# Attention scores of six half sequences: two heads at once in TensorE's row halves

## The chip, the cores and the metric

The kernel runs on one core of a Trainium2 chip. The metric is the time of one execution on the device in microseconds (us), lower is better. Before the change it is 242.82 us, the median of three runs (242.07 to 243.31); the profiled execution has a span of 239.8 us.

A core has five engines that run beside each other: TensorE (PE) multiplies matrices, VectorE (DVE), ScalarE (ACT) and GpSimd (POOL) work on elements, and SyncE (SP) mostly starts transfers. Each takes its instructions in program order, and waits on semaphores where it needs another engine's result. TensorE writes into PSUM, which here is cut into eight banks of 128 x 512 fp32; ScalarE and VectorE read them.

## What is computed

Attention with a local window and a few global keys, and then a feed-forward layer with two gates on its result:

```python
def _attn_ref(q, k, v, n_global, n_local):          # q, k, v: 4 x 8 heads x 768 x 64
    scores = scale * np.matmul(q, k.transpose(0, 1, 3, 2))
    ...
    keep = is_global | is_local                     # 8 global keys, the last 96 keys
    bias = -slopes[:, None, None] * dist[None, :, :]
    scores = np.where(keep, scores + bias[None, :, :, :], -1000000000.0)
    a = softmax(scores)
    return np.matmul(a, v)

def _moe_ref(x, w_gate, w_val, w_out):              # x: 3072 x 512, inner width 1536
    gate = np.maximum(x @ w_gate, 0.0)
    return gate * (x @ w_val) @ w_out
```

## The kernel before, in words

**Halves.** Each of the four sequences of 768 positions is cut into two halves of 384 queries; the kernel numbers them s = 0 to 7, and this text says half one to half eight. Half one is s = 0. The feed-forward layer of a half c has 24 products of its first stage (a gate and a value product for each of 12 blocks, L700: four matmuls of 384 columns each), then the second stage (L733 in full, or L590, which forms the product of two row blocks from seven smaller products, with sums of h and of weights that VectorE makes, L556 and L583 to L586). ScalarE applies the relu to a gate product (L709), VectorE multiplies the value product by it (L716, `ht`).

**The weave.** There is no scheduler: engines run in the order in which the code records instructions. `weave` goes through the feed-forward products of half c and records, at set fractions of their number, the pieces of attention of half c+1 (`attention_pieces`) and of the preparation of half c+2 (`early_pieces`). So a TensorE instruction of an attention piece that waits holds up all feed-forward products behind it. Halves one and two are done by other functions in a start-up section. Half three's pieces lie in the products of halves one and two, half four's to seven's in 0.88 of the products of the half before, half eight's in 0.8 of them.

**Attention of a half.** Heads come in pairs p = 0 to 3, with e = 0, 1 for the head in the pair. Keys lie in tiles j of 128 rows, the 8 global keys first. A half touches four or five tiles, each with w of 128 query columns in three groups; they are sorted into three groups g of a PSUM bank each (`banks_of_half`).
- *Scores* (`piece_qk`, L410): both heads of a pair in one matmul. The 128 rows of the stationary operand are the keys of both heads, 64 dimensions each. The queries `qTb` are padded: for e = 0 rows 64 to 127 are zero, for e = 1 rows 0 to 63. The result has 2·3·w columns. One bank of the pool `qk_psum` (three banks) per group.
- *Exp* (L413) reads the bank and writes `es` as bf16; *masks* (`piece_mask`, L428) multiply it on VectorE with the bias factors. The masks of one piece are recorded behind the exp of the next.
- *Values* (`piece_av`, L444): four or five matmuls per head into a bank of `av_psum` (two banks, in turn). 64 of their rows are the values, 64 the sums of weights. ScalarE takes the logarithm of the sums (L453), and after the second head of a pair the inverse by an exp (L458, `rcp`).
- *Normalization* (`piece_norm`, L464): VectorE multiplies each head's values by `rcp` into `xT`. This frees the head's `av_psum` bank.

The feed-forward products take the other three banks (`ff_psum`).

**Order of pieces.** For a half, `attention_pieces` gives 26 pieces: scores of pairs 0 and 1 (three pieces each), values of pair 0 (two), its second normalization, scores of pair 2, values of pair 1, and so on. Each scores piece records one group's matmuls and its exp.

**Preparation** (`early_pieces`): GpSimd casts keys and queries to bf16 (L366, L374; the query casts go into the padded `qz`), transposing transfers bring them to `kNb` and `qTb` (L377, L381), and GpSimd puts keys in their order (`piece_order`). For half three, TensorE transposes (`T2_piece`), and ScalarE copies the queries into the padded layout (L312).

Of the kernel before, what the change touches and what calls it, by code (L numbers as in the profile page):

```python
# [8 lines left out]
FP32 = mybir.dt.float32  # L9
BF16 = mybir.dt.bfloat16  # L10
FP16 = mybir.dt.float16
AF = mybir.ActivationFunctionType
# [4 lines left out]
def kernel(  # L17
# [12 lines left out]
    nc = tc.nc  # L30

    B, H, S, D = q.shape
    NG = int(n_global)
    NL = int(n_local)
    DM = H * D
# [3 lines left out]
    HP = H // 2  # L39
    QH = S // 2  # L40
    NN = 3
    KT = 128 - NG
    PK = KT // NN
    WQ = 72
    NHALF = 2 * B
    NT = -(-S // KT)
    scale = 1.0 / math.sqrt(D)
# [5 lines left out]
    banks_of_half = [[], []]  # L53
    spans = []
    for half in range(2):
        for j in range(NT):
            w0 = PK * j - 128 * half
            a, b_ = max(0, w0), min(128, w0 + WQ)
# [7 lines left out]
    const = ctx.enter_context(tc.tile_pool(name="const", bufs=1))  # L66
    setupp = ctx.enter_context(tc.tile_pool(name="setupp", bufs=1))
    stage = ctx.enter_context(tc.tile_pool(name="stage", bufs=1))
    es_pool = ctx.enter_context(tc.tile_pool(name="es", bufs=3))
    rc_pool = ctx.enter_context(tc.tile_pool(name="rc", bufs=2))  # L70
    xt_pool = ctx.enter_context(tc.tile_pool(name="xt", bufs=3))
    ht_pool = ctx.enter_context(tc.tile_pool(name="ht", bufs=2))
# [14 lines left out]
    kT = [[const.tile([128, NT, 128], BF16, name=f"kT{i}_{p}") for p in range(HP)] for i in range(2)]  # L87
    qTb = [const.tile([128, HP, 2, QH], BF16, name=f"qT{i}") for i in range(2)]
    kNb = [const.tile([128, HP, QH], BF16, name=f"kN{i}") for i in range(2)]
    qz = [const.tile([128, NN, HP, 2, 128], BF16, name=f"qz{i}") for i in range(2)]  # L90
    kc = [const.tile([128, NN, DM], BF16, name=f"kc{i}") for i in range(2)]

    obuf = const.tile([128, 2, 5, DM // 2], FP32)
# [7 lines left out]
    m_all = const.tile([128, H, 2, NN, WQ], BF16)  # L101
# [141 lines left out]
    def warm_up(n):  # L243
        wps = ff_psum.tile([128, 512], FP32, name="ff_ps")
        for _ in range(n):
            nc.tensor.matmul(wps, lhsT=warm, rhs=warm.unsqueeze(1).to_broadcast([128, 4, 128]), start=True, stop=True)

    xT_of = {}
    es_of = {}
    es01_of = {}  # L250
    av_of = {}

    cast_of = {}
# [55 lines left out]
    def piece_copy_q(s, p, copy=nc.vector.tensor_copy):  # L309
        for e in range(2):  # L310
            r = slice(64 * e, 64 * e + 64)
            copy(qTb[s % 2][r, p, e, :], tp_of[s, p, 0][r, :])  # L312
# [32 lines left out]
    def piece_exp(s, p, g):  # L345
        if p == HP - 1:

            es = kNb[s].rearrange("d p t -> d (p t)")[:, 480 * g : 480 * (g + 1)]
        else:
            if g == 0:  # L350
                es01_of[s, p] = es_pool.tile([128, 2, 480], BF16, name="es01")
            es = es01_of[s, p][:, g] if g < 2 else es_pool.tile([128, 480], BF16, name="es2")
        c = 0
        for j, a, w, m in banks_of_half[s % 2][g]:
            for e in range(2):
                es_of[s, p, j, e] = (es, c)
                c += NN * w
        nc.scalar.activation(es[:, 0:c], qk_of[s, p][g][:, 0:c], AF.Exp, bias=0.0, scale=scale)  # L358
# [3 lines left out]
        for g in range(3):  # L362
            piece_exp(s, p, g)

    def piece_cast_k(s, p):
        nc.gpsimd.tensor_copy(  # L366
            kc[s % 2].rearrange("t n (h d) -> t h n d", d=D)[:, 2 * p : 2 * p + 2],
            ks_of[s][:, 2 * p : 2 * p + 2, :].rearrange("t e (n d) -> t e n d", n=NN))

    def piece_cast_q(s, p):  # L370

        qsrc = qs_of[s][:, 2 * p : 2 * p + 2, :].rearrange("t e (n d) -> t e n d", n=NN)
        for e in range(2):
            nc.gpsimd.tensor_copy(qz[s % 2][:, :, p, e, 64 * e : 64 * e + 64], qsrc[:, e])  # L374

    def piece_xk(s, n):
        nc.sync.dma_start_transpose(  # L377
            out=kNb[s % 2][:, :, n * 128 : (n + 1) * 128], in_=kc[s % 2][:, n])

    def piece_xq(s, n):  # L380
        nc.sync.dma_start_transpose(  # L381
            out=qTb[s % 2].rearrange("d p e t -> d (p e) t")[:, :, n * 128 : (n + 1) * 128],
            in_=qz[s % 2][:, n].rearrange("t p e z -> t (p e z)"))

    def piece_order(s, p):
        b, half = divmod(s, 2)
        put_keys(nc.gpsimd.tensor_copy, nc.gpsimd.tensor_copy, kT[b % 2][p], kNb[s % 2][:, p], half)

    def early_pieces(s):
        out = [(0.0, lambda p=p: piece_cast_k(s, p)) for p in range(HP)]  # L390
        out += [(0.0, lambda n=n: piece_xk(s, n)) for n in range(NN)]
        out += [(0.0, lambda p=p: piece_cast_q(s, p)) for p in range(HP)]
        out += [(0.0, lambda n=n: piece_xq(s, n)) for n in range(NN)]
        out += [(0.0, lambda p=p: piece_order(s, p)) for p in range(HP)]
        return out

    def piece_qk(s, p, g, later=None):
        b, half = divmod(s, 2)
        kt = kT[b % 2][p]
        qd = qTb[s % 2][:, p].rearrange("d e (n p) -> d e n p", n=NN)  # L400
        bank = banks_of_half[half][g]
        cols = sum(2 * NN * w for _, _, w, _ in bank)
        ps = qk_psum.tile([128, 512], FP32, name="qk_ps")
        if g == 0:
            es01_of[s, p] = es_pool.tile([128, 2, 480], BF16, name="es01")
        es = es01_of[s, p][:, g] if g < 2 else es_pool.tile([128, 480], BF16, name="es2")
        c = 0
        for j, a, w, m in bank:
            n_ = 2 * NN * w
            nc.tensor.matmul(ps[:, c : c + n_], lhsT=kt[:, j, :],  # L410
                             rhs=qd[:, :, :, a : a + w], start=True, stop=True)
            c += n_
        nc.scalar.activation(es[:, 0:cols], ps[:, 0:cols], AF.Exp, bias=0.0, scale=scale)  # L413
        if later is None:
            piece_mask(s, p, bank, es)
        else:
            later.append(lambda: piece_mask(s, p, bank, es))
# [15 lines left out]
    def piece_av(s, p, e):  # L433
        b, half = divmod(s, 2)
        h = 2 * p + e
        vb = vbuf[b % 2]
        av = av_psum.tile([128, 512], FP32, name="av_ps")
        av_of[s, p, e] = av
        av3 = av[:, 0:QH].rearrange("d (n p) -> d n p", n=NN)
        todo = [t for bank in banks_of_half[half] for t in bank]  # L440
        for i, (j, a, w, m) in enumerate(todo):
            es, c = es_of[s, p, j, e]
            z0 = 2 * D * h + (D if e == 0 else 0)
            nc.tensor.matmul(av3[:, :, a : a + w],  # L444
                             lhsT=vb[:, j, z0 : z0 + 128],
                             rhs=es[:, c : c + NN * w].rearrange("k (n p) -> k n p", n=NN),
                             start=(i == 0), stop=(i == len(todo) - 1),
                             skip_group_check=True)
        o0, d0 = (0, 64) if e == 0 else (64, 0)
        if e == 0:  # L450
            av_of[s, p, "l"] = rc_pool.tile([128, QH], FP32, name="lnd")
        ln = av_of[s, p, "l"]
        nc.scalar.activation(ln[o0 : o0 + 64], av[d0 : d0 + 64, 0:QH], AF.Ln, bias=0.0, scale=1.0)  # L453
        if e == 1:
            if s not in xT_of:
                xT_of[s] = xt_pool.tile([128, N_DC, QH], BF16, name="xT")
            rc = rc_pool.tile([128, QH], FP32, name="rcp")
            nc.scalar.activation(rc, ln, AF.Exp, bias=0.0, scale=-1.0)  # L458
            av_of[s, p, "r"] = rc
            piece_norm(s, p, 0)  # L460
# [43 lines left out]
    def piece_mul_wide(s, p):  # L504
        if s not in xT_of:
            xT_of[s] = xt_pool.tile([128, N_DC, QH], BF16, name="xT")
        nc.vector.tensor_tensor(xT_of[s][:, p, :], av_of[s, p][1][:, 0:QH], av_of[s, p, "r"], op=ALU.mult)  # L507

    def attention_pieces(s):
        masks = []  # L510

        def qk(p, g):
            ready = masks[:]
            masks.clear()
            piece_qk(s, p, g, masks)
            for f in ready:
                f()

        def flush():
            for f in masks:  # L520
                f()
            masks.clear()

        QK = lambda p: [(0.18, lambda g=g: qk(p, g)) for g in range(3)]
        AV = lambda p: [(0.29, lambda e=e: (flush(), piece_av(s, p, e))) for e in range(2)]
        N = lambda p: [(0.0, lambda: piece_norm(s, p, 1))]
        g = QK(3)
        a = AV(2)
        return (QK(0) + QK(1) + AV(0) + N(0) + QK(2) + AV(1) + N(1) + g[0:1] + a[0:1] + g[1:3] + a[1:2]
                + N(2) + [(0.0, lambda: None)] * 2 + AV(3) + N(3))  # L530


    out_v = out.rearrange("(s p n) d -> s n p d", p=128, n=NN)
# [156 lines left out]
    def ffn_pieces(c):  # L690
# [63 lines left out]
        if c == NHALF - 2:  # L754
            return f1, pair.items({"1": late[0:2], "2": late[2:4]})

        space = qz[0].rearrange("t n p e z -> t (n p e z)").bitcast(FP16)
        across = Pair((c - 1, 2), (c, 2), space.rearrange("t (s c z) -> t s c z", s=4, c=NP))
        sums = across.sums(0, NP)
        return f1, (pair.items({"1": late[0:2], "2": late[2:4], "4": sums[0:1], "6": sums[1:2], "5": sums[2:4]})  # L760
# [32 lines left out]

    for h in range(H):
        setup_sid(h)
    QKB, FFB, AVB = (qk_psum, "qk_ps"), (ff_psum, "ff_ps"), (av_psum, "av_ps")

    def AV(s, p, *pools):
        piece_av_wide(s, p, *pools)
        piece_norm_wide(s, p)  # L800
# [130 lines left out]
        nc.gpsimd.memset(kT[1][p][:, 3, 32:128].bitcast(mybir.dt.uint32), 0)  # L931
        nc.gpsimd.memset(kT[1][p][:, 6, NG + 48 : 128].bitcast(mybir.dt.uint32), 0)
    nc.gpsimd.memset(vbuf[1][:, NT - 1, :].bitcast(mybir.dt.uint32), 0)
    for i in range(2):
        nc.gpsimd.memset(qz[i].rearrange("t n p e z -> t (n p e z)").bitcast(mybir.dt.uint32), 0)
    for j in range(NT):
        fill_ones(nc.gpsimd, 1, j)
    for p in range(HP):
# [3 lines left out]
    def T2_piece(p):  # L942
        piece_t(2, p, *QKB, apart=True)
        piece_copy_k(2, p)
        piece_copy_q(2, p, nc.scalar.copy)

    T2 = [(0.0, lambda p=p: T2_piece(p)) for p in range(HP)]
    weave(f1_1[G[0]] + f1_0[G[1]][4:] + f1_1[G[1]],
# [54 lines left out]
```

The softmax here doesn't subtract the row's maximum and nothing guards it: scores larger than these inputs give would overflow.

## Time and profile before

| engine | busy, us | share of the span |
|---|---|---|
| TensorE matmuls | 232.1 | 97% |
| VectorE | 174.8 | 73% |
| ScalarE | 154.3 | 64% |
| GpSimd | 95.6 | 40% |

| group | count | mean of one, ns |
|---|---|---|
| gate and value products, 128 x 384 (L700) | 768 | 326 |
| scores (L410) | 118 | 286 |
| values (L444) | 216 | 226 |
| exp of scores, 128 x 432 (L413) | 38 | 531 |
| logarithm (L453) | 48 | 485 |
| inverse (L458) | 24 | 523 |
| normalization (L464) | 48 | 555 |
| h product (L716) | 96 | 554 |

The mean of a matmul is its time from start to end; the next one starts before it ends, so counts times means is more than TensorE's busy time. Busy time alone doesn't say what bounds: for that the chain of waits is read, which goes back from the last instruction to what released each one. TensorE's granted clock is 1.00 over the whole span. In the timeline a row is a start, a duration, the engine, the line and the tiles, and in brackets the idle time ahead of it and what ended it.

### The profile page before, as it was taken

The numbers are of one execution on the slowest core, as the hardware profiler recorded it, in microseconds if no ns is written. First come the engines' busy times: TensorE is split into PE (matmuls) and PEld (weight loads), VectorE is DVE, ScalarE is ACT, GpSimd is POOL, SyncE is SP. The second block draws the span as 40 slices with busy tenths as digits, with TensorE's granted clock in tenths as the row PEclk, the third lists the DMA queues.
The fourth block names the chain that finished last, engine by engine and source line by source line (L and its number), as shares of the span: only waits on it lengthen the run. The fifth ranks groups of instructions, "written<-read, shape, count | busy, mean of one in ns | idle before, by whom it ended". The sixth has DMA issues, their size and how long they took to land.

```text
span 239.8 us, 5192 instructions
## 1 busy us (share of the span) xinstructions
PE 232.1 (97%) x1859; PEld 155.9 (65%) x1859; DVE 174.8 (73%) x443; ACT 154.3 (64%) x328; POOL 95.6 (40%) x213
## 2 busy tenths in 40 slices
PE   7889999999999999999999999999999999999992
PEld 3676756666558666766658666676658666866682
DVE  6878676767877778585985778675985867964783
ACT  7899856878662787548754787547764888433300
POOL 8998935915590068103484066502460000000000
PEclk9999999999999999999999999999999999999999
DMA  6999999997989946938569756929451200020004
GB/s 171 197 173 185 205 282 261 171 103 253 129 178 148 305 122 133 93 94 258 92 112 128 224 159 154 110 68 290 69 131 45 90 0 3 0 87 3 0 26 151
DMA packets 78329, 32.37 MB, mean 135 GB/s; under 512 B 55424, under 2 KB 76928, under 8 KB 78304
## 3 DMA queue, kind: packets, MB, share of 16 engines
q0 software_dynamic: 34896, 10.27, 38.1%
q1 hardware_dynamic: 43408, 21.78, 34.3%
q8 instruction: 14, 0.23, 0.4%
q14 instruction: 11, 0.09, 0.1%
HBM read 28.38 MB, written 6.29 MB: 145 GB/s over the span
## 4 chain that ended last, share of the span: by engine, by line
PE 89%; ACT 4%; DMA 2%; DVE 1%; SPq 1%; issue 0%; DVEq 0%; ACTq 0%
PE ff_ps L700 51%; PE ff_ps L590 15%; PE ff_ps L733 9%; PE qk_ps L410 6%; PE av_ps L444 6%; DMA qs<-in_q_dram 2%; ACT es L358 2%; SPq L116 1%; PE av_ps L479 1%; PE qk_ps L296 1%; ACT es L413 1%; PE qk_ps L479 1%; DVE obuf L601 0%; ACT kN L358 0%; ACT grelu L709 0%; DVE xT L507 0%
## 5 line engine op out<-in xcount | busy, mean ns | idle before, releaser
L700 PE MATMUL ff_ps<-xT,wv 128*128 128x384 bf16 x384 | 77.7, 326 | 0.1
L700 PE MATMUL ff_ps<-xT,wg 128*128 128x384 bf16 x384 | 77.7, 325 | 0.0
L709 ACT ACTIVATE grelu<-ff_ps 128x384 bf16<-128x384 f32 x96 | 46.9, 491 | 45.3 <-PE ff_ps L700 32.6
L716 DVE TENSOR_TENSOR ht<-ff_ps,grelu 128x384 f16<-128x384 f32 x96 | 53.1, 554 | 24.4 <-PE ff_ps L700 12.8
L700 PEld LDWEIGHTS <-wv 128*128 128x128 bf16 x384 | 36.2, 97 | 22.3 <-DMA wv<-in_moe_w_val_dram 0.4
L700 PEld LDWEIGHTS <-wg 128*128 128x128 bf16 x384 | 36.0, 97 | 20.9 <-issue 0.5
L464 DVE TENSOR_TENSOR xT<-av_ps,rcp 64x384 bf16<-64x384 f32 x48 | 26.7, 555 | 24.9 <-ACT rcp L458 24.0
L413 ACT ACTIVATE es<-qk_ps 128x432 bf16<-128x432 f32 (+2 forms) x78 | 40.9, 534 | 5.5 <-PE qk_ps L410 3.5
L428 DVE TENSOR_TENSOR es<-es,m_all 128x432 bf16<-128x432 bf16 (+5 forms) x118 | 32.9, 322 | 0.2
L366 POOL CAST kc<-ks 128x384 bf16<-128x384 f32 x20 | 9.4, 517 | 57.9 <-DMA ks<-in_k_dram 57.9
L453 ACT ACTIVATE lnd<-av_ps 64x384 f32<-64x384 f32 x48 | 23.3, 485 | 8.9 <-PE av_ps L444 8.5
L410 PE MATMUL qk_ps<-qT,kT 128*128 128x432 bf16 (+5 forms) x118 | 26.6, 286 | 0.1
L151 POOL DMA_DIRECT2D vbuf<-in_v_dram x29 | 24.8, 863 | 0.1
L601 DVE TENSOR_TENSOR obuf<-ff_ps,obuf 128x512 f32<-128x512 f32 (+1 forms) x35 | 20.5, 592 | 4.3 <-PE ff_ps L590 2.0
L733 PE MATMUL ff_ps<-wo_sb,ht 128*128 128x512 f16 x96 | 22.8, 378 | 0.0
L444 PEld LDWEIGHTS <-vbuf 128*128 128x128 bf16 x216 | 18.3, 98 | 6.8
L444 PE MATMUL av_ps<-es,vbuf 128*128 128x216 bf16 (+4 forms) x216 | 21.4, 226 | 0.0
L590 PEld LDWEIGHTS <-hsum 128*128 128x128 f16 x168 | 16.4, 98 | 2.0
L410 PEld LDWEIGHTS <-kT 128*128 128x128 bf16 x118 | 11.4, 98 | 7.7
L590 PE MATMUL ff_ps<-wo_sum,hsum 128*128 128x256 f16 x126 | 14.9, 273 | 0.0
L590 PEld LDWEIGHTS <-ht 128*128 128x128 f16 x144 | 13.7, 97 | 1.8
L733 PEld LDWEIGHTS <-ht 128*128 128x128 f16 x96 | 8.7, 97 | 8.7
(125 smaller groups left out, 245.7 us busy)
## 6 DMA issues: line engine op xcount, KB each, us to landing
out_dram<-obuf SPq DMA_DIRECT2D x22, 256.0 KB
ks<-in_k_dram SPq DMA_DIRECT2D x5, 768.0 KB
qs<-in_q_dram SPq DMA_DIRECT2D x5, 768.0 KB
vbuf<-in_v_dram POOLq DMA_DIRECT2D x23, 120.0 KB, 4.8
wv<-in_moe_w_val_dram POOLq DMA_DIRECT2D x3, 512.0 KB, 9.8
wo_sb<-in_moe_w_out_dram POOLq DMA_DIRECT2D x1, 1536.0 KB, 21.1
wg<-in_moe_w_gate_dram POOLq DMA_DIRECT2D x2, 512.0 KB, 9.7
ks<-in_k_dram SPq DMA_DIRECT2D x4, 192.0 KB
```

The lines of the kernel that those rows point to most:

```text
L151: nc.gpsimd.dma_start(out=v_dst(b, NG + r0, NG + r0 + n, j), in_=v[b, :, KT * j + r0 : KT * j + r0 + n, :].rearrange("h p d -> p h d"))
L410: nc.tensor.matmul(ps[:, c : c + n_], lhsT=kt[:, j, :], rhs=qd[:, :, :, a : a + w], start=True, stop=True)
L413: nc.scalar.activation(es[:, 0:cols], ps[:, 0:cols], AF.Exp, bias=0.0, scale=scale)
L428: nc.vector.tensor_mul(e4, e4, mk)
L444: nc.tensor.matmul(av3[:, :, a : a + w], lhsT=vb[:, j, z0 : z0 + 128], rhs=es[:, c : c + NN * w].rearrange("k (n p) -> k n p", n=NN), star ...
L453: nc.scalar.activation(ln[o0 : o0 + 64], av[d0 : d0 + 64, 0:QH], AF.Ln, bias=0.0, scale=1.0)
L464: nc.vector.tensor_tensor(xT_of[s][r, p, :], av_of[s, p, e][r, 0:QH], av_of[s, p, "r"][r], op=ALU.mult)
L590: nc.tensor.matmul(ps[:, c0 : c0 + DH], lhsT=lhs(i), rhs=rhs(i), start=(i == 0), stop=(i == NP - 1), skip_group_check=True)
L700: nc.tensor.matmul(st[key][:, 0:QH], lhsT=w_of(w, dc, fc), rhs=xT_of[c][:, dc, :], start=(dc == 0), stop=(dc == N_DC - 1))
L709: nc.scalar.activation(gr, psg[:, 0:QH], AF.Relu, bias=0.0, scale=1.0)
L716: nc.vector.tensor_tensor(ht[:, fc, :], psv[:, 0:QH], st["r", fc], op=ALU.mult)
L733: nc.tensor.matmul(ps2, lhsT=ht[:, fc, n * 128 : (n + 1) * 128], rhs=wo_sb[:, fc, :], start=(fc == 0), stop=(fc == N_FC - 1))
```

## The change

For halves three to eight the scores are no longer formed from a pair's 128 rows with padded queries. Each head's 64 rows are a matmul of their own, on rows 0 to 63 for e = 0 and 64 to 127 for e = 1, with the queries of that head alone (3·w columns instead of 2·3·w). The two matmuls of a pair use different row halves of TensorE and write different banks, so they can run at the same time. That is what it is for: to spare TensorE the zero half of the padded products.

A unit of scores (`score_unit`) now covers two groups for two banks each, four PSUM banks: one of `av_psum` and the three of `qk_psum`. There are three units per half, each recorded in one piece, and 12 exps, one per bank, in pieces of their own (`unit_exp`). A bank holds the same head e of two pairs (heads 4pp + e and 4pp + e + 2) instead of both heads of one pair; the masks take the two heads with a step of two. The order of a half's pieces becomes 27:

```
X(U0) X X X wait X(U1) X X a0 X a0 N0 X(U2) X a1 X X a1 N1 AV2 N2 wait wait AV3 N3
```

where X(Uk) records unit k and the first of its exps, X another exp, a0 and a1 the values of one head of pairs 0 and 1, AV both heads, N the second normalization. The queries lose their padding: one cast per pair instead of two on GpSimd, half the bytes in the query transposes, one copy instead of two in `T2_piece`, no zeroing of `qz`. The exp tiles become a pool of 12 buffers of 128 x 480.

```diff
-    es_pool = ctx.enter_context(tc.tile_pool(name="es", bufs=3))
+    es_pool = ctx.enter_context(tc.tile_pool(name="es", bufs=12))
...
-    qz = [const.tile([128, NN, HP, 2, 128], BF16, name=f"qz{i}") for i in range(2)]
+    qT2 = [qTb[1].rearrange("d p e t -> d (p e t)")[:, i * HP * QH : (i + 1) * HP * QH].rearrange(
+        "d (p t) -> d p t", p=HP) for i in range(2)]
+    qc = [const.tile([128, NN, DM], BF16, name=f"qc{i}") for i in range(2)]
...
+    def score_unit(s, groups, pools):
+        b, half = divmod(s, 2)
+        out = []
+        for pp, g in groups:
+            banks = []
+            for e in range(2):
+                pool, name = pools.pop(0)
+                banks.append(pool.tile([128, 512], FP32, name=name))
+                out.append((pp, g, e, banks[e]))
+            c = 0
+            for j, a, w, m in banks_of_half[half][g]:
+                for p in (2 * pp, 2 * pp + 1):
+                    for e in range(2):
+                        r = slice(64 * e, 64 * e + 64)
+                        q3 = qT2[s % 2][r, p].rearrange("d (n p) -> d n p", n=NN)
+                        nc.tensor.matmul(banks[e][:, c : c + NN * w], lhsT=kT[b % 2][p][r, j, :],
+                                         rhs=q3[:, :, a : a + w], start=True, stop=True)
+                    c += NN * w
+        return out
...
-        QK = lambda p: [(0.18, lambda g=g: qk(p, g)) for g in range(3)]
...
-        return (QK(0) + QK(1) + AV(0) + N(0) + QK(2) + AV(1) + N(1) + g[0:1] + a[0:1] + g[1:3] + a[1:2]
-                + N(2) + [(0.0, lambda: None)] * 2 + AV(3) + N(3))
+        U = [([(0, 0), (0, 1)], (AVB, QKB, QKB, QKB)),
+             ([(0, 2), (1, 0)], (AVB, QKB, QKB, QKB)),
+             ([(1, 1), (1, 2)], (AVB, QKB, QKB, QKB))]
+        X = lambda u=None: [(0.0, lambda: x(u))]
...
+        return (X(U[0]) + X() + X() + X() + wait + X(U[1]) + X() + X() + a0[0:1] + X() + a0[1:2] + N(0)
+                + X(U[2]) + X() + a1[0:1] + X() + X() + a1[1:2] + N(1) + AV(2) + N(2) + wait * 2 + AV(3) + N(3))
...
-    for i in range(2):
-        nc.gpsimd.memset(qz[i].rearrange("t n p e z -> t (n p e z)").bitcast(mybir.dt.uint32), 0)
...
-        piece_copy_q(2, p, nc.scalar.copy)
+        nc.scalar.copy(qT2[0][:, p], tp_of[2, p, 0])
```

More of the change, by code (lines that the diff above doesn't have):

```diff
@@ L246, in warm_up @@
             nc.tensor.matmul(wps, lhsT=warm, rhs=warm.unsqueeze(1).to_broadcast([128, 4, 128]), start=True, stop=True)
+    QKB, FFB, AVB = (qk_psum, "qk_ps"), (ff_psum, "ff_ps"), (av_psum, "av_ps")
     xT_of = {}
     es_of = {}
-    es01_of = {}
     av_of = {}
@@ L349, in piece_exp @@
         else:
-            if g == 0:
-                es01_of[s, p] = es_pool.tile([128, 2, 480], BF16, name="es01")
-            es = es01_of[s, p][:, g] if g < 2 else es_pool.tile([128, 480], BF16, name="es2")
+            es = es_pool.tile([128, 480], BF16, name="es")
         c = 0
@@ L363, in piece_biased, with piece_cast2, piece_x @@
             piece_exp(s, p, g)
-    def piece_cast_k(s, p):
+    def piece_cast2(s, p, dst, src):
         nc.gpsimd.tensor_copy(
[L367 to L383, printed above, removed]
+            dst[s % 2].rearrange("t n (h d) -> t h n d", d=D)[:, 2 * p : 2 * p + 2],
+            src[s][:, 2 * p : 2 * p + 2, :].rearrange("t e (n d) -> t e n d", n=NN))
+    def piece_x(dst, src, n):
+        nc.sync.dma_start_transpose(out=dst[:, :, n * 128 : (n + 1) * 128], in_=src[:, n])
     def piece_order(s, p):
@@ L389, in early_pieces @@
     def early_pieces(s):
[L390 to L393, printed above, removed]
+        out = [(0.0, lambda p=p: piece_cast2(s, p, kc, ks_of)) for p in range(HP)]
+        out += [(0.0, lambda n=n: piece_x(kNb[s % 2], kc[s % 2], n)) for n in range(NN)]
+        out += [(0.0, lambda p=p: piece_cast2(s, p, qc, qs_of)) for p in range(HP)]
+        out += [(0.0, lambda n=n: piece_x(qT2[s % 2], qc[s % 2], n)) for n in range(NN)]
         out += [(0.0, lambda p=p: piece_order(s, p)) for p in range(HP)]
@@ L403, in piece_qk @@
         ps = qk_psum.tile([128, 512], FP32, name="qk_ps")
-        if g == 0:
-            es01_of[s, p] = es_pool.tile([128, 2, 480], BF16, name="es01")
-        es = es01_of[s, p][:, g] if g < 2 else es_pool.tile([128, 480], BF16, name="es2")
+        es = es_pool.tile([128, 480], BF16, name="es")
         c = 0
@@ L507, in piece_mul_wide, with unit_exp, mask @@
         nc.vector.tensor_tensor(xT_of[s][:, p, :], av_of[s, p][1][:, 0:QH], av_of[s, p, "r"], op=ALU.mult)
-    def attention_pieces(s):
[L510 to L517, printed above, removed]
+    def score_unit(s, groups, pools):
[17 more added lines that the diff above has]
+        return out
+    def unit_exp(s, pp, g, e, ps):
+        bank = banks_of_half[s % 2][g]
+        cols = sum(2 * NN * w for _, _, w, _ in bank)
+        es = es_pool.tile([128, 480], BF16, name="es")
+        nc.scalar.activation(es[:, 0:cols], ps[:, 0:cols], AF.Exp, bias=0.0, scale=scale)
+        def mask():
+            c = 0
+            for j, a, w, m in bank:
+                n_ = 2 * NN * w
+                e4 = es[:, c : c + n_].rearrange("k (i n p) -> k i n p", i=2, n=NN)
+                h0 = 4 * pp + e
+                mk = m_all[:, h0 : h0 + 3 : 2, 0 if j == 0 else 1, :, m : m + w]
+                if w == WQ:
+                    e4 = e4.rearrange("k i n p -> k i (n p)")
+                    mk = mk.rearrange("k i n p -> k i (n p)")
+                nc.vector.tensor_mul(e4, e4, mk)
+                for i in range(2):
+                    es_of[s, 2 * pp + i, j, e] = (es, c + i * NN * w)
+                c += n_
+        return mask
+    def attention_pieces(s):
+        masks, units = [], []
         def flush():
@@ L522, in flush, with scores, x @@
             masks.clear()
-        QK = lambda p: [(0.18, lambda g=g: qk(p, g)) for g in range(3)]
-        AV = lambda p: [(0.29, lambda e=e: (flush(), piece_av(s, p, e))) for e in range(2)]
+        def scores(groups, pools):
+            units.extend(score_unit(s, groups, list(pools)))
+        def x(scored=None):
+            ready = masks[:]
+            masks.clear()
+            if scored:
+                scores(*scored)
+            masks.append(unit_exp(s, *units.pop(0)))
+            for f in ready:
+                f()
+        U = [([(0, 0), (0, 1)], (AVB, QKB, QKB, QKB)),
+             ([(0, 2), (1, 0)], (AVB, QKB, QKB, QKB)),
+             ([(1, 1), (1, 2)], (AVB, QKB, QKB, QKB))]
+        X = lambda u=None: [(0.0, lambda: x(u))]
+        AV = lambda p: [(0.0, lambda e=e: (flush(), piece_av(s, p, e))) for e in range(2)]
         N = lambda p: [(0.0, lambda: piece_norm(s, p, 1))]
-        g = QK(3)
-        a = AV(2)
-        return (QK(0) + QK(1) + AV(0) + N(0) + QK(2) + AV(1) + N(1) + g[0:1] + a[0:1] + g[1:3] + a[1:2]
-                + N(2) + [(0.0, lambda: None)] * 2 + AV(3) + N(3))
+        wait = [(0.0, lambda: None)]
+        a0, a1 = AV(0), AV(1)
+        return (X(U[0]) + X() + X() + X() + wait + X(U[1]) + X() + X() + a0[0:1] + X() + a0[1:2] + N(0)
+                + X(U[2]) + X() + a1[0:1] + X() + X() + a1[1:2] + N(1) + AV(2) + N(2) + wait * 2 + AV(3) + N(3))
     out_v = out.rearrange("(s p n) d -> s n p d", p=128, n=NN)
@@ L755, in ffn_pieces @@
             return f1, pair.items({"1": late[0:2], "2": late[2:4]})
-        space = qz[0].rearrange("t n p e z -> t (n p e z)").bitcast(FP16)
+        space = qTb[0].rearrange("d p e t -> d (p e t)").bitcast(FP16)
         across = Pair((c - 1, 2), (c, 2), space.rearrange("t (s c z) -> t s c z", s=4, c=NP))
@@ L795 @@
         setup_sid(h)
-    QKB, FFB, AVB = (qk_psum, "qk_ps"), (ff_psum, "ff_ps"), (av_psum, "av_ps")
     def AV(s, p, *pools):
```

## The prediction

> **What bounds the kernel now.** I read the busy table first, then the chain that ended last, then the costliest groups, and last the timeline around the places that the change touches.
>
> ```profile
> PE 232.1 (97%) x1859; PEld 155.9 (65%) x1859; DVE 174.8 (73%) x443; ACT 154.3 (64%) x328; POOL 95.6 (40%) x213
> ...
> PE 89%; ACT 4%; DMA 2%; DVE 1%; SPq 1%; issue 0%; DVEq 0%; ACTq 0%
> ...
> L410 PE MATMUL qk_ps<-qT,kT 128*128 128x432 bf16 (+5 forms) x118 | 26.6, 286 | 0.1
> ```
>
> TensorE is the bound: 89% of the chain, and from 22 us to 235 us the chain is nothing but its matmuls. The 286 ns of a score matmul (L410) is latency and overlaps the next one; its cost is the spacing of starts. Four 384-column matmuls of a gate or value product take 0.65 us (the rows at 144.29 and 144.93 below), 2.36 columns per ns, issue included. From 45 to 236 us I compared all starts with that rate: 189.4 us of matmul and 0.85 us of anything else. So TensorE has no slack: work taken off it shortens the kernel, and every wait put in front of it lengthens it.
>
> The change gives TensorE new waits on the accumulator banks of the values product (AVB, two banks), so the chain that frees such a bank matters. In half six (timeline, 144 us; start, duration):
>
> ```profile
> 143.98 0.47 PE L444 MATMUL av_ps<-es,vbuf 128*128 128x72 bf16 x5
> 144.29 0.81 PE L700 MATMUL ff_ps<-xT,wg 128*128 128x384 bf16 x4
> 144.48 0.48 ACT L453 ACTIVATE lnd<-av_ps 64x384 f32<-64x384 f32 x1 [0.26 <-PE av_ps L444]
> 144.93 0.81 PE L700 MATMUL ff_ps<-xT,wv 128*128 128x384 bf16 x4
> 145.00 0.52 ACT L458 ACTIVATE rcp<-lnd 128x384 f32<-128x384 f32 x1
> 145.55 0.55 DVE L464 TENSOR_TENSOR xT<-av_ps,rcp 64x384 bf16<-64x384 f32 x1 [0.28 <-ACT rcp L458]
> 146.03 0.54 DVE L716 TENSOR_TENSOR ht<-ff_ps,grelu 128x384 f16<-128x384 f32 x1
> 146.49 0.41 DVE L584 TENSOR_TENSOR hsum<-hsum,ht 128x512 f16<-128x512 f16 x1
> 146.93 0.56 DVE L464 TENSOR_TENSOR xT<-av_ps,rcp 64x384 bf16<-64x384 f32 x1
> 147.09 0.47 PE L444 MATMUL av_ps<-es,vbuf 128*128 128x72 bf16 x5
> ```
>
> The second head's product leaves TensorE at 144.29. Logarithm, inverse and normalization free the first head's bank at 146.10 (1.81 us later), the second's at 147.49 (3.20 us later; an h product and an h sum stand between the two normalizations on VectorE). The next product here starts after 2.80 us and the one behind it after 6.1 us, so neither waits. In the last half the margin is already thin:
>
> ```profile
> 196.93 0.81 PE L700 MATMUL ff_ps<-xT,wv 128*128 128x384 bf16 x4
> ...
> 198.41 0.55 DVE L464 TENSOR_TENSOR xT<-av_ps,rcp 64x384 bf16<-64x384 f32 x1 [1.36 <-ACT rcp L458]
> ...
> 199.08 0.47 PE L444 MATMUL av_ps<-es,vbuf 128*128 128x72 bf16 x5
> ```
>
> The product ends at 196.93, its bank is free at 198.96, the next product starts at 199.08.
>
> **What the Trainium skill says.** "TensorEngine Tiling (Array Packing)", Key Properties: tiles work independently and in parallel, and changing the tiling mode drains TensorE. The same page, Gotcha 1: row tiles must not write one PSUM bank together, hence two banks per group. "TensorE: Matmul & The Clock Gate", Part 3: tiles start some 4 ns apart, and four row tiles were measured at 3.07 times. The kernel before has no row tiles but has column halves (L479), which agree on both points:
>
> ```profile
> 25.54 0.48 PE L479 MATMUL av_ps<-es,vbuf 128*64 128x72 bf16 x10
> 25.85 0.48 PE L479 MATMUL qk_ps<-es,ones 128*64 128x72 bf16 x10
> 26.16 0.48 PE L479 MATMUL qk_ps<-es,vbuf 128*64 128x72 bf16 x10
> 26.57 0.50 PE L700 MATMUL ff_ps<-xT,wv 128*128 128x384 bf16 x2
> ```
>
> Ten matmuls of 1392 columns take 0.31 us from start to start, where one after the other would take 0.59: two at once. After the last ten, full matmuls should start at 26.47 and start at 26.57: 0.10 us lost. On the way in (28.53 expected, 28.62 seen) 0.09.
>
> **The change, part by part.**
> *Scores.* A pair of heads has 2·3·(72+72+48+8) = 1200 score columns in the first half of a sequence (halves three, five, seven), 2·3·(24+64+72+56+16) = 1392 in the second. Four pairs and three halves of each kind make 31,104 columns: 13.2 us at 2.36 per ns. With two at once, priced by the column halves (0.28 us for 1200 columns at 12.86 us, 0.31 for 1392): 12·0.28 + 12·0.31 = 7.1 us. Gain 6.1.
> *Mode changes.* Three units per half, six halves, in and out: 36 × 0.095 = 3.4 us lost. For row tiles the trace shows no price; bounds are 0 and this, and I take this since the cause named is the drain.
> *Weight loads.* 216 instead of 108, two per pair of matmuls. Full 24-column matmuls, each with its own load, start 26 to 28 ns apart, so two loads may need 52 ns: that binds only for pairs of 24, 48 and 72 columns, at most 0.8 us in all; at least 0. I take 0.4.
> *Exp and masks.* The same number of exps and mask products over the same columns (L413, L428); only the heads are paired otherwise. No change in work, but four banks now fill at once, and ScalarE empties them in runs of 0.53 to 0.57 us each between relus of 0.49 (L709), so a logarithm comes later than now.
> *Casts, memsets, transposes, the copy of queries.* POOL loses half of L374's casts and 2.7 us of L935's memsets, ScalarE four of eight L312 copies (0.47 us each), queues half of the query transposes. At no cost or gain: no score matmul waited for them (L410: 0.1 us idle), and TensorE is full beside them.
> *The exp tiles* grow to 12: hidden, nothing waited for them.
> *New waits.* Each unit takes one AVB bank and three QKB. AVB goes round two banks: unit 1, unit 2, the two products of pair 0, unit 3, and so on. QKB waits fall away in my walk (last exp of a unit ends 0.1 to 0.9 us before the next unit's matching bank). AVB waits don't. I count the matmul groups of 0.65 us between the product that starts the chain and the one that needs the bank, and add to 1.81 and 3.20 what ScalarE is late.
> - Halves four to seven. Unit 3: three groups, 1.95 us, against 1.81 plus 0.2 late (a relu and an exp still stand ahead of the logarithm): 0.1, which overlaps the drain, so 0. First product of pair 2: 1.95 against 1.9: 0. Its second product: 1.95 + 0.28 + 0.65 = 2.9 us against 3.2 plus 0.1 late, plus up to 0.26 where the h sum takes 0.67 us (as L586 at 149.64): 0.6, bounds 0.3 to 0.8. VectorE's queue holds normalization, h product (which waits for a relu behind the inverse), h sum, normalization. Four halves: 2.4 us.
> - Half three. Unit 3 stands two groups (1.3 us) after the product, against 1.81 plus 0.45 late: 0.95, less the drain 0.9. (Late: 0.65 us after the first product ScalarE ends a relu, then logarithm, exp and relu take 1.5; the second product has ended after 1.57, and 0.19 later its logarithm could start.) First product of pair 2: 1.3 against 1.85: 0.55. Second: a weight sum (0.61, L556) stands between the normalizations: 0.25. Sum 1.7.
> - Half eight, where the pieces are packed into 0.8 of the products. Unit 3: two groups, 1.3 against 1.81 plus 0.3: 0.75 without the drain. First product of pair 2: only one group, 0.65, against 1.81 plus 0.5: 1.6 us. (Late: from unit 3's first full bank ScalarE has four exps, three relus and a logarithm, 4.4 us, while TensorE reaches the end of the second product 4.45 us after unit 3 starts, its bank full after 0.5.) Sum 2.35.
> Behind each stands all of TensorE, so nothing hides them: 6.45 us.
> *Sum.* −6.1 + 3.4 + 0.4 + 6.45 = +4.1: 242.8 becomes 246.9.
>
> **Rivals.**
> *A, faster.* The AVB waits nearly vanish because the chain runs ahead of my walk. For it: ScalarE and VectorE are busy only 64% and 73%. Against: the 1.81 us are four dependent steps, not queueing, and 0.65 us lies between two of them in half eight. −6.1 + 3.4 = −2.7: 240.1.
> *B, row halves cost no drain.* Then −6.1 + 6.75 (the waits no longer overlap drains) = +0.6: 243.4. For: no row-tile price is in the trace. Against: both directions of column halves cost the same 0.095.
> *C, the halves don't run together,* because both banks or the weight loads serialize them: nothing gained, 246.9 + 6.1 = 253. Against: column halves reach the full factor.
>
> **How the numbers follow.** Forecast 0.65, A 0.12, B 0.17, C 0.06. Predicted is the forecast's 246.9. The waits' bounds (4.5 to 7.5), drains and loads put the forecast between 244.5 and 248.5. The range 241.8 to 249 leaves out most of A, C and the tail. Faster (under 241.6): A and a little of B, 0.14. Within 0.5% (to 244.0): most of B, some of the forecast's lower end, 0.17. Slower: 0.69.
>
> **What would show it.** Score matmuls in pairs 3 to 4 ns apart; about 0.095 us extra at each border of the 18 units; TensorE idle ahead of values products in the chain, released by the normalization, near 0.6 us once in each of the halves four to seven, and 1.6 us once in half eight. I am wrong if these products start right behind the group ahead, or if the borders cost nothing.

## The result, and the profile after

The changed kernel takes 244.72 us (median of four runs, 244.56 to 245.69); the kernel before takes 242.44 us in the runs beside it (241.73 to 243.31). The ratio is 1.0101, with a 95% interval of 1.0056 to 1.0145: slower by 1.4 to 3.5 us. The spans of the two profiled executions are 242.9 and 239.8 us.

The page of the changed kernel, with the rows that answer to those of before: busy times, the chain that ended last, and the values products (busy time, mean ns of one, idle time ahead of them and what ended it).

```profile
PE 231.5 (95%) x1967; PEld 152.4 (63%) x1967; DVE 176.1 (73%) x443; ACT 149.4 (62%) x324; POOL 90.2 (37%) x191
...
PE 71%; DVE 10%; POOL 7%; DMA 4%; ACT 4%; issue 2%; POOLq 0%; DVEq 0%; ACTq 0%
...
L431 PE MATMUL av_ps<-es,vbuf 128*128 128x216 bf16 (+4 forms) x216 | 21.5, 226 | 3.0 <-DVE xT L451 3.0
```

GpSimd lost 5.4 us of busy time, ScalarE 4.9. The chain of before has no GpSimd and from 22 us on nothing but matmuls, and the first score of half three comes no earlier than before (48.3 against 47.7 us), so nothing of this came back. TensorE's share of the chain fell from 89% to 71% and VectorE's rose from 1% to 10%. Part of this is the start: there the chain of after goes through GpSimd and a transfer of weights (7% and 4%) up to 30.6 us, where that of before is on matmuls from 22 us on. Behind the start it now passes again and again through logarithm, inverse and normalization. These shares say where the chain runs, not how long TensorE stood still; that is counted below. The third row names one place: before a values product, TensorE stood idle until a normalization (L451, line 464 of before) had freed a bank.

Two places of the timeline show both sides of the change. The first unit of scores:

```profile
47.91 0.49 PE L740 MATMUL ff_ps<-xT,wv 128*128 128x384 bf16 x2
48.33 0.26 PE L513 MATMUL av_ps<-qT,kT 64*128 64x216 bf16 x1
48.34 0.26 PE L513 MATMUL qk_ps<-qT,kT 64*128 64x216 bf16 x1
...
48.81 0.82 PE L740 MATMUL ff_ps<-xT,wg 128*128 128x384 bf16 x4
```

The two row halves start together (3 to 5 ns apart in 102 of 108 pairs; "TensorE: Matmul & The Clock Gate", Part 3, of the Trainium skill says some 4 ns of tiles). Two matmuls of 0.1625 us from 47.91 on would end the full mode at 48.235; the first score starts at 48.33, 0.095 us later: the mode change. Eight matmuls of 216 columns then take 0.48 us up to the next full matmul, the way out included, where one after the other they would take 0.74.

And half eight, where the pieces stand closest:

```profile
201.77 0.47 PE L431 MATMUL av_ps<-es,vbuf 128*128 128x72 bf16 x5
...
202.08 0.81 PE L740 MATMUL ff_ps<-xT,wv 128*128 128x384 bf16 x4
...
202.48 0.48 ACT L440 ACTIVATE lnd<-av_ps 64x384 f32<-64x384 f32 x1
203.00 0.52 ACT L445 ACTIVATE rcp<-lnd 128x384 f32<-128x384 f32 x1
203.55 1.14 DVE L451 TENSOR_TENSOR xT<-av_ps,rcp 64x384 bf16<-64x384 f32 x2 [0.56 <-ACT rcp L445]
...
204.16 0.48 PE L431 MATMUL av_ps<-es,vbuf 128*128 128x72 bf16 x5 [1.27 <-DVE xT L451]
```

One value product of the feed-forward layer (202.08) stands between the second head's product of pair 1 and the first of pair 2. The bank comes free only behind logarithm, inverse and normalization, and TensorE waits.

To see where all of the time went, I took the starts of all matmuls from the first score of half three to the last matmul, and compared each with the pace of a full matmul. Full matmuls of 256, 384 and 512 columns start 109, 162 and 216 ns apart, which a line of columns / 2.4 + 2.5 ns fits; those of 24 and 48 columns start 28 ns apart, and what this is above the line stands in both columns under smaller gaps. Scores of the changed kernel are counted from the first start of a unit to the last one and its pace. What is beyond the pace at a border between modes is a mode change up to 0.095 us; the rest, where over 0.03 us, is a wait.

| from first score to last matmul, us | before | after |
|---|---|---|
| score matmuls | 13.23 | 7.17 |
| mode changes (35) | 0 | 3.25 |
| waits | 0.45 | 5.82 |
| smaller gaps | 0.40 | 0.66 |
| gate and value products | 102.70 | 102.70 |
| values products | 13.50 | 13.50 |
| second stage | 57.29 | 57.29 |
| sum | 187.57 | 190.39 |

So the stretch is 2.82 us longer, in one execution of each kernel. The medians differ by 2.3. Of the difference 0.3 lies outside the span: device time less span is 2.10 us in the runs of before and 1.78 in those of after. What these 0.3 us are stays open; the rest is within the spread of single executions. The first score comes at 47.3 to 48.6 us in all kernels of this study, with no order that follows their edits.

### The profile page after: what moved, and what is told of

Its sections match the earlier page's. It is cut to its first block, busy times and chain, and to the rows that moved or that the text cites. A ratio compares the mean times of both kernels' runs of the same rounds, so it can differ in the third digit from the quotient of the medians.

```text
span 242.9 us, 5373 instructions
## 1 busy us (share of the span) xinstructions
PE 231.5 (95%) x1967; PEld 152.4 (63%) x1967; DVE 176.1 (73%) x443; ACT 149.4 (62%) x324; POOL 90.2 (37%) x191
## 4 chain that ended last, share of the span: by engine, by line
PE 71%; DVE 10%; POOL 7%; DMA 4%; ACT 4%; issue 2%; POOLq 0%; DVEq 0%; ACTq 0%
PE ff_ps L740 40%; PE ff_ps L630 14%; PE ff_ps L773 8%; PE av_ps L431 4%; DMA wv<-in_moe_w_val_dram 4%; DVE ht L756 3%; POOL vbuf L154 2%; PE av_ps L513 2%; DVE xT L451 2%; DVE es L534 2%; PE qk_ps L513 2%; DVE obuf L641 1%; POOL kc L131 1%; ACT rcp L445 1%; ACT lnd L440 1%
## 5 line engine op out<-in xcount | busy, mean ns | idle before, releaser
L740 PEld LDWEIGHTS <-wg 128*128 128x128 bf16 x384 | 36.6, 98 | 21.9 <-issue 0.7
L740 PEld LDWEIGHTS <-wv 128*128 128x128 bf16 x384 | 35.6, 98 | 23.3 <-issue 1.4
L451 DVE TENSOR_TENSOR xT<-av_ps,rcp 64x384 bf16<-64x384 f32 x48 | 26.6, 555 | 20.2 <-ACT rcp L445 19.5
L534 DVE TENSOR_TENSOR es<-es,m_all 128x432 bf16<-128x432 bf16 (+3 forms) x108 | 31.1, 330 | 1.5 <-ACT es L522 1.4
L367 POOL CAST kc<-ks 128x384 bf16<-128x384 f32 x20 | 10.0, 541 | 57.7 <-DMA ks<-in_k_dram 50.1
L522 ACT ACTIVATE es<-qk_ps 128x432 bf16<-128x432 f32 (+2 forms) x54 | 27.8, 531 | 0.1
L431 PEld LDWEIGHTS <-vbuf 128*128 128x128 bf16 x216 | 17.6, 98 | 12.1 <-DVE xT L451 5.8
L445 ACT ACTIVATE rcp<-lnd 128x384 f32<-128x384 f32 x24 | 12.5, 523 | 0.8
L630 PE MATMUL ff_ps<-wo_sb,ht 128*128 128x256 f16 x96 | 11.8, 272 | 0.0
```

The source lines that it names most:

```text
L431: nc.tensor.matmul(av3[:, :, a : a + w], lhsT=vb[:, j, z0 : z0 + 128], rhs=es[:, c : c + NN * w].rearrange("k (n p) -> k n p", n=NN), star ...
L451: nc.vector.tensor_tensor(xT_of[s][r, p, :], av_of[s, p, e][r, 0:QH], av_of[s, p, "r"][r], op=ALU.mult)
L534: nc.vector.tensor_mul(e4, e4, mk)
L630: nc.tensor.matmul(ps[:, c0 : c0 + DH], lhsT=lhs(i), rhs=rhs(i), start=(i == 0), stop=(i == NP - 1), skip_group_check=True)
L740: nc.tensor.matmul(st[key][:, 0:QH], lhsT=w_of(w, dc, fc), rhs=xT_of[c][:, dc, :], start=(dc == 0), stop=(dc == N_DC - 1))
```

## The experiments

All times are medians beside runs of the kernel before on the same chip. "Waits" and "mode changes" are those of the table.

**The row halves in turn.** All matmuls of row half 0 of a unit are recorded first, then all of row half 1.

```diff
-        for pp, g in groups:
-            ...
-                for p in (2 * pp, 2 * pp + 1):
-                    for e in range(2):
+        for e in range(2):
+            for k, (pp, g) in enumerate(groups):
+                ...
+                    for p in (2 * pp, 2 * pp + 1):
```

> The changed kernel with the loops of a unit turned: first all matmuls on row half 0, then all on row half 1. The same instructions, banks and mode changes, but the two row halves can run together only where they meet, once per unit. Theory (the row halves save about 6 us of TensorE because pairs run together): the score matmuls go from 7.2 us back to about 12.4 us, and the time rises by about 5 us to 249.9. Rival (the matmuls of 64 rows cost less by themselves, whether they run together or not): within 1 us of the changed kernel.

Measured: 247.71 us, ratio 1.0229 (1.0190 to 1.0268), score time 10.03 us. That is 2.86 us more than in the changed kernel, about half of what was expected. The timeline of this kernel tells why:

```profile
51.14 0.31 PE L514 MATMUL av_ps<-qT,kT 64*128 64x144 bf16 x3
51.29 0.23 PE L514 MATMUL qk_ps<-qT,kT 64*128 64x144 bf16 x1
51.31 0.17 PE L514 MATMUL av_ps<-qT,kT 64*128 64x24 bf16 x1
```

The order recorded for this unit is four matmuls into `av_ps`, two of 216 columns into `qk_ps` (all row half 0), and only then row half 1, whose first is a matmul of 144 columns into `qk_ps`. That one, recorded seventh, starts at 51.29, before the fourth (51.31) and the two of 216. In units of eight equal matmuls row half 1 even starts 13 ns behind row half 0 (47.30 and 47.31). In all 18 units the first matmul of row half 1, recorded fifth, seventh or ninth, starts 8 to 13 ns after the matmul recorded four places ahead of it: it overtakes three that wait, and no more. So the order in the code did not take the overlap away; it took part of it. As a test of the gain it was not clean, and the next one takes its place.

**Both heads on one row half.** The odd heads' scores are left out: their matmuls run on the even heads' rows, in the same number, shape and order.

```diff
-                        r = slice(64 * e, 64 * e + 64)
+                        r = slice(0, 64)
```

> The changed kernel with all score matmuls on row half 0: the scores of the odd heads are left out and those of the even heads formed twice. The same number of matmuls, columns, banks and mode changes, and no two can run together. Theory (the gain of the row halves is that pairs run together): the score matmuls take 13.2 us instead of 7.2, 6 us more, 250.7. Rival (a matmul of 64 rows is cheaper by itself): within 1.5 us of the changed kernel.

Measured: 252.03 us, ratio 1.0427 (1.0389 to 1.0466). Score time 14.02 us, waits 6.24.

```profile
48.16 0.26 PE L513 MATMUL av_ps<-qT,kT 64*128 64x216 bf16 x1
48.26 0.25 PE L513 MATMUL qk_ps<-qT,kT 64*128 64x216 bf16 x1
48.35 0.25 PE L513 MATMUL av_ps<-qT,kT 64*128 64x216 bf16 x1
```

The same matmuls now start 0.09 us apart, 216 columns at full pace, instead of two at a time. The score time is 6.85 us longer than in the changed kernel, and 0.8 longer than that of the padded matmuls of before, which are half as many: a matmul of 64 rows is not cheaper by itself. The gain in the scores is the pairing.

**Twice the mode changes.** One full matmul of 24 columns between the two groups of each unit: 18 more ways out and in.

```diff
+            if (pp, g) == groups[0]:
+                nc.tensor.matmul(banks[1][:, 488:512], lhsT=ident, rhs=ident[:, 0:24], start=True, stop=True)
```

> The changed kernel with one full matmul of 24 columns between the two groups of each unit, into unused columns of a bank (its result is read by nobody). 18 more places where TensorE goes from row halves to full and back. Theory (each change of the tiling mode costs 0.095 us): 18 x (0.19 + 0.015) = 3.7 us more than the changed kernel, 248.4. Rival (the 0.09 us at the borders is the way from a semaphore or from the other queue's order, not the mode): 0.3 to 0.5 us more.

Measured: 249.63 us, ratio 1.0307 (1.0277 to 1.0336).

```profile
47.96 0.25 PE L513 MATMUL qk_ps<-qT,kT 64*128 64x216 bf16 x1
48.14 0.19 PE L517 MATMUL qk_ps<-ident 128*128 128x24 bf16 x1
48.26 0.36 PE L513 MATMUL qk_ps<-qT,kT 64*128 64x216 bf16 x4
```

From the last pair to the small matmul 0.18 us pass, 0.09 more than 216 columns take; from there to the next pair 0.12, where full matmuls of 24 columns follow each other after 0.028: again 0.09 more. The 71 mode changes add up to 6.62 us instead of 3.25, 0.093 each. The waits grew by 0.6 us and the small matmuls take 0.23; the stretch is 4.6 us longer in all, as the first pair behind each border is slower too (0.2 us in sum, see below). The price of a mode change is shown, for row halves too.

**The fourth h sum one block later.** In halves four to seven VectorE has an h sum between the two normalizations of pair 1. Its place is taken from it.

```diff
-            if c > 1 and 7 <= fc < N_FC - 1:
+            if c > 1 and fc in (7, 8, 9, 11):
                 ...
-                first[0][fc - 7]()
+                first[0][min(fc - 7, 3)]()
```

> The changed kernel with the fourth h sum (L626) of a half recorded one block later on VectorE, so that it no longer stands between the two normalizations of pair 1. Theory (in halves four to seven the second product of pair 2 waits about 0.5 us for a normalization behind normalization, h product and h sum): these four waits fall by the 0.41 to 0.67 us of the sum, to 0 to 0.15 us each, and the time by about 1.7 us to 243.0. Rival (the wait is set by the logarithm and the inverse on ScalarE): unchanged within 0.4 us.

Measured: 242.78 us, ratio 1.0028 (1.0017 to 1.0038); waits 4.19 us instead of 5.82. In half four, the changed kernel first:

```profile
96.01 0.61 DVE L626 TENSOR_TENSOR hsum<-ht,hsum 128x512 f16<-128x512 f16 x1
...
96.64 0.56 DVE L451 TENSOR_TENSOR xT<-av_ps,rcp 64x384 bf16<-64x384 f32 x1
...
97.25 0.48 PE L431 MATMUL av_ps<-es,vbuf 128*128 128x72 bf16 x5 [0.38 <-DVE xT L451]
```

and with the later sum:

```profile
95.30 0.54 DVE L756 TENSOR_TENSOR ht<-ff_ps,grelu 128x384 f16<-128x384 f32 x1
...
95.85 0.56 DVE L451 TENSOR_TENSOR xT<-av_ps,rcp 64x384 bf16<-64x384 f32 x1
...
96.47 0.48 PE L431 MATMUL av_ps<-es,vbuf 128*128 128x72 bf16 x5
```

The normalization follows the h product at once, and the product has no idle time ahead of it. One VectorE instruction of 0.4 to 0.6 us, four times, was 1.6 of the 5.8 us.

**Pieces at set places.** If the waits come from the packing, placing the pieces farther apart should take them away.

```diff
-        return (X(U[0]) + X() + X() + X() + wait + X(U[1]) + ...
+        at = [(1, X(U[0])), (2, X()), (3, X()), (4, X()), (6, X(U[1])), (7, X()), (8, X()),
+              (9, a0[0:1]), (10, a0[1:2]), (11, X()), (11.1, N(0)),
+              (14, X(U[2])), (15, X()), (15.05, a1[0:1]), (16, X()), (17, a1[1:2]), (18, X()), (18.1, N(1)),
+              (21, a2[0:1]), (22.5, a2[1:2]), (23.6, N(2)), (27, a3[0:1]), (29, a3[1:2]), (30.1, N(3))]
...
-            placed.append(spread(attention_pieces(c + 1), 0.0, 0.88 if c + 2 < NHALF else 0.8))
+            placed.append(place(attention_pieces(c + 1), 0.0, 0.88))
```

> The changed kernel with its attention pieces at set places instead of even ones: unit 3 four products after the second product of pair 0 instead of two or three, the first product of pair 2 four products after the second of pair 1, and so on; half eight in 0.88 of the products like the others. The same instructions per engine. Theory (5.4 us of the time are waits of TensorE for an AVB bank, set by the chain logarithm, inverse, normalization): nearly all of these waits go, the mode changes stay, so about 239.5 us, 5 us less than the changed kernel and 2.5 to 3 us less than the kernel before. Rival (ScalarE and VectorE are as a whole too slow for pieces in bunches, so that the wait moves to another piece): within 1.5 us of the changed kernel.

Measured: 244.95 us, ratio 1.0114 (1.0089 to 1.0138); waits 6.09 us. The waits for normalizations are gone and others took their place, which is the outcome that the rival named:

```profile
92.62 0.51 ACT L522 ACTIVATE es<-qk_ps 128x432 bf16<-128x432 f32 x1
...
93.03 0.48 ACT L753 ACTIVATE grelu<-ff_ps 128x384 bf16<-128x384 f32 x1
...
93.56 0.48 PE L744 MATMUL ff_ps<-xT,wg 128*128 128x384 bf16 x2 [0.48 <-ACT grelu L753]
```

Exps, a relu and two logarithms stand close together on ScalarE (1.94 of the 2 us from 90 to 92), the inverse and one more exp right behind them, so a relu comes late, its `ff_psum` bank is not free, and the next gate product waits. Seven waits ahead of gate and value products, from 0.38 to 0.77 us, make 4.1 us. Nearly all of the other 2 us stand ahead of the last matmul or two of a values product, and the trace names a mask (L534) for the longer ones: the wait that the next run shows was there already. That ScalarE and VectorE are as a whole too slow, which was the rival's reason, is not shown by this, and the last experiment speaks against it.

**Pieces at other places.** The same edit, with the exps between values products rather than beside them: U0 at 1, exps at 2, 3, 4, U1 at 6, exps at 7 and 8, a0 at 9 and 11, an exp at 13, U2 at 15, exps at 16.5, 19 and 22 between a1 at 18 and 20, a2 at 24 and 25, a3 at 29 and 30, of 35 places; in half eight pairs 2 and 3 stand at 23, 24, 27 and 28, of 31.

> The changed kernel with its attention pieces at set places, chosen for both limits: four products between the second product of pair 0 and unit 3, four between the second of pair 1 and the first of pair 2, pairs 2 and 3 in the second stage of the layer (where no relus are), and exps and logarithms of the first stage spread so that ScalarE has at most about 10 us of them beside 6 us of relus in its 17 us. The same instructions per engine. Theory (AVB waits cost 5.4 us; the spaced version put them off AVB but bunched exps, so that gate and value products waited for relus): the waits of TensorE fall from 5.8 to under 1.5 us, so about 240.3 us, 1.5 to 2.5 us below the kernel before, of 6.1 - 3.4 = 2.7 us that the row halves leave after the mode changes. Rival (units of four banks make more exps per stretch than ScalarE can empty, wherever they stand): waits of 4 us or more, 243.5 us or more.

Measured: 243.37 us, ratio 1.0038 (1.0021 to 1.0054); waits 4.86 us. The time expected was missed by 3 us. The long waits ahead of gate and value products are gone but for one (0.61, in half eight's stretch); new ones lie inside the second product of pair 2, in half four:

```profile
94.73 0.56 DVE L451 TENSOR_TENSOR xT<-av_ps,rcp 64x384 bf16<-64x384 f32 x1
...
95.33 0.56 DVE L762 TENSOR_TENSOR ht<-ff_ps,grelu 128x384 f16<-128x384 f32 x1
...
95.80 0.38 DVE L534 TENSOR_TENSOR es<-es,m_all 128x432 bf16<-128x432 bf16 x1
...
96.23 0.27 PE L431 MATMUL av_ps<-es,vbuf 128*128 128x216 bf16 x1 [0.34 <-DVE es L534]
```

The last matmul of the product needs the mask of the half's last exp. Masks are recorded behind the next exp; the last one has none, so it was recorded only with the first product of pair 2, behind a normalization and an h product on VectorE. In halves three to seven this cost 0.44 to 0.66 us each, and half eight had 1.6 us of waits of its own, its pieces being late.

**The mask ahead, with the later h sum.** The last mask gets a piece of its own (`flush`), the last exp stands a little earlier, half eight's places lie closer to its start, and the h sum is later.

```diff
+        a2, a3, F = AV(2), AV(3), [(0.0, flush)]
...
+            at = [..., (18.8, X()), (20, a1[1:2]), (21.1, N(1)), (21.2, X()), (22.6, F), (24, a2[0:1]), ...]
```

> The pieces at set places again, but the mask of a half's last exp now has a piece of its own, more than one block ahead of the values products of the third pair, the last exp stands a little earlier, half eight's pieces lie closer to its start, and the fourth h sum is one block later. Theory: what was left of the waits in the run with the set places was this mask behind VectorE's normalization and h product (0.44 to 0.66 us in each of halves three to seven, 2.6 us in all) and half eight's late tail (1.6 us); with both gone TensorE waits for at most 1.5 us from the first score on, and the time is near 239.9 us, 0.99 of the kernel before. Rival: ScalarE and VectorE have no place left for the earlier exps and the mask, so the wait moves to the relus or the h products, as in the first spaced run: 4 us of waits or more, 243 us and no better than before.

Measured: 240.61 us (239.63 to 241.27), ratio 0.9928 (0.9903 to 0.9953); waits 1.91 us. It is faster than both kernels. The rows that answer to those of the changed kernel:

```profile
PE 230.4 (96%) x1967; PEld 152.8 (64%) x1967; DVE 175.8 (74%) x443; ACT 149.0 (62%) x324; POOL 89.6 (37%) x191
...
PE 82%; POOL 7%; DMA 4%; DVE 3%; issue 1%; ACT 1%; POOLq 0%; DVEq 0%
...
L431 PE MATMUL av_ps<-es,vbuf 128*128 128x216 bf16 (+4 forms) x216 | 21.4, 226 | 0.0
```

No values product waits any more, with every matmul of the change in place and the mode changes still 3.24 us. Of the waits left, 1.45 us lie in half eight (an h product late for a matmul of the second stage that starts at 205.51, and a normalization late for one of a gate product that starts at 210.75). How much each of the edits in it brings was not run; of them only the h sum was measured alone.

## Why the prediction was right, and by how much it was off

It said slower, by four terms. Against the stretch of the table:

| step of the prediction, us | predicted | measured |
|---|---|---|
| scores, two heads at once | −6.1 | −6.06 |
| 36 mode changes | +3.4 | +3.35 (35 in the stretch and the first way in) |
| weight loads | +0.4 | none seen (whatever they cost is in the scores) |
| AVB waits, half three | +1.7 | +1.54 |
| AVB waits, halves four to seven | +2.4 | +2.16 |
| AVB waits, half eight | +2.35 | +1.94 |
| smaller gaps | not named | +0.26 |
| waits of feed-forward products that before had | not named | −0.27 |

- **Scores and mode changes** came out to 0.1 us, although both prices were taken from column halves (L479 of before). The experiments with one row half and with twice the mode changes show each by itself.
- **Weight loads.** The step gave two loads up to 52 ns and took the middle of its bounds (0 to 0.8). Pairs of 24, 48 and 72 columns, two loads each, start 25 to 39 ns apart, and those of 24 columns 25 to 29, no more than full matmuls of 24 columns with one load (28 or 29). The scores take 7.17 us where the price without this term was 7.1, so all or nearly all of the 0.4 was too much.
- **AVB waits** were named right in cause and nearly everywhere in place, and were sized 0.8 us too large in sum. By place: at the second product of pair 2 0.55 and 0.52 in halves four and five and 0.41 and 0.44 in halves six and seven (predicted 0.6), where 0.14 and 0.10 stand at the first product already (predicted 0); unit 3 of half three 0.72 (0.9), its two products of pair 2 0.67 and 0.15 (0.55 and 0.25); in half eight unit 3 0.50 (0.75) and the first product of pair 2 1.44 (1.6). The step that was mis-sized most there is how late ScalarE is in half eight, which I added to the 1.81 us from the second head's product to the free bank: 0.3 at unit 3 and 0.5 at pair 2. The products leave TensorE at 195.80 and 202.08 us, and the normalizations that free the bank end at 197.65 and 204.11, after 1.85 and 2.03 us: ScalarE was late by 0.04 and 0.22.
- **Left out of the sum** were two things that cancel. The waits of feed-forward products that before had (0.45 us) are 0.18 after. The smaller gaps grew by 0.26; 0.19 of it is that the first full matmul behind each of the 18 units takes 10 to 11 ns longer than its pace. The first pair of a unit is as much slower (102 to 104 ns for 216 columns instead of 92), so a border costs a little more than the gap.
- **The remainder.** The steps above give 4.1 us predicted and 2.82 measured; the medians show 2.3, since 0.3 us went outside the span, which no step foresaw. The measured 244.72 lies at the low end of the 244.5 to 248.5 that the forecast gave itself.
- **The rivals.** That the waits nearly vanish (A) fell for this order of pieces: 5.64 us of them stood in front of TensorE. It was not wrong in kind: with the pieces at other places ScalarE and VectorE do have room, and the time of the last experiment, 240.61, is close to the 240.1 that A gave, for another order of pieces, so A is not confirmed by it. That row halves cost no drain (B) and that they don't run together (C) fell with the doubled mode changes and with the single row half. B's figure lay nearest to the measured time, 243.4 against 244.72, next to the forecast's 246.9: a time near a rival's is no evidence for its mechanism.

## What to carry to other kernels

When TensorE is full, a layout that halves its work on one stage is worth the halved time less the borders: count how often it switches, times the price of a border, before counting anything else. Then follow each bank from the instruction that fills it to the one that frees it, through every queue on the way, and give each of these steps (a sum, a mask recorded late, a relu behind exps) its distance; the same matmuls took 244.7 or 240.6 us here by where the pieces and one sum stood. A fix that moves one wait can bring up another engine's, so read the waits anew after each placing.

## What the runs showed of the hardware that was not expected

- Matmuls on different row halves don't keep the recorded order of their starts: a matmul of row half 1, recorded seventh, started ahead of the fourth to sixth, of row half 0 (51.288 us against 51.308, 51.333 and later). So what the text ahead of the prediction says, that each engine takes its instructions in program order, does not hold for these starts. In the 18 units of that run a matmul overtakes at most three that are recorded ahead of it; whether the bound is the same in other kernels was not tried. Turning the loops so that all of row half 0 is recorded first cost only 2.86 of the 6.85 us that losing the overlap costs.
- A border between full matmuls and row halves costs the same as one with column halves, 0.09 to 0.1 us in either direction, and it stays the same when only 24 columns stand between two borders. The first matmuls behind it are 10 to 12 ns slower besides.
- The two weight loads of a pair on two row halves add nothing that shows: pairs of 24 columns start 25 to 29 ns apart, full matmuls of 24 columns 28 or 29.
